# A retention-plus-MLP kernel whose order is laid out by a planner: new rule for fetched TensorE instructions, new table of moves, a bank-marking matmul moved to the head of its group, and another gate for w_out

## The chip, the cores and the metric

The kernel runs on one core of one Trainium2 chip. The metric is the device time of one execution in microseconds (us); the median of three runs before the change is 287.15 us (286.87 to 288.31). Engines are called PE (TensorE, the matrix engine), PEld (its weight loads, which overlap its matmuls), DVE (VectorE), ACT (ScalarE), POOL (GpSimd) and SP (SyncE, which here issues transfers only). Lines are named as in the kernel before: L983 is line 983.

## The reference

Inputs are float32: q, k and v of shape 8 x 8 x 576 x 64 (batch, heads, positions, width), w_in 512 x 2048 and w_out 2048 x 512. The output is 4608 x 512 in float32.

```python
scores = (1/sqrt(64)) * q @ k.transpose            # per batch and head
gamma  = 1 - 2 ** (-5 - head)
ret    = scores * where(row >= col, gamma ** (row - col), 0)
x      = (ret @ v) laid out as 4608 tokens x 512   # heads side by side
h      = x @ w_in                                  # 4608 x 2048
out    = (h * cos(h)) @ w_out                      # 4608 x 512
```

## The kernel before

**Units of attention.** The 576 positions of a batch are cut into units of 256 positions (four chunks of 64) and a remainder of 64. For one unit the kernel loads q, k and v into staging tiles (`stgq`, `stgk`, `stgv`; `load`, L537), scales or casts them to bf16 (`qnat`, `natk`, `natv`; `unit`, L548), turns q and k round (`tpe` on PE for the first four units, a transposing DMA, `txb`, for the others), makes masked scores inside the chunks and a running state across them (`scores`, `states`, `snap`), and from both the unit's rows of x, in bf16, in `xt` (`outputs`, L734). All these are short matmuls of 64 rows, and all of them are recorded at L650.

**Blocks of the MLP.** The 4608 tokens make nine blocks of 512; two units fill one block. For blocks 0 to 3 the first product is plain (`mlp1`, matmuls at L854). For blocks 4 to 8 it is one level of a Strassen-Winograd scheme with seven products in place of eight (`seven1`, matmuls at L983, four groups per block, 20 in all). The second product takes that scheme for all nine blocks (`wino2`, matmuls at L1123). h * cos(h) is made by ACT (cosine) and by DVE or POOL (product), L863 to L866 and L966 to L972.

**A group of `seven1`.** It holds three of the eight PSUM banks: A, Bb and C. Product 1 is accumulated in A. Then ACT copies A to Bb (`seed`, L912, recorded at L914), and product 2 adds onto that copy in Bb. For the adding to work, a matmul must have written the whole of Bb as its last use; the list `whole` keeps for each bank whether that is so. Where it isn't, `mark` (L471, recorded at L472) puts one matmul of ones of 512 columns on that bank, ahead of ACT's copy. The copy waits for it.

**What sets the order.** `graph` (L1180) lists some 1,400 tasks, each with an engine, a duration by estimate, and a due time. `shift` (L217) adds to the due times a table of corrections, `SHIFT` (L370): each three characters of it are a step to the next task that is moved, and a move of up to 40 us either way. `run` (L235) then plays the tasks on five engines in estimated time, and takes at each step a task that can start soonest and has the smallest due time; this gives the order in every queue, and the banks and buffers. So each engine's queue on the chip is a fixed list, and waits are by semaphores. A slot of a pool of buffers (`bk` is the PSUM banks) is picked at L333: the one that came free first.

**The fetch of PE's instructions in the planner.** `pick` has a rule (L270 to L273): PE's instructions come in blocks of 256; a block is asked for when PE has come to a certain instruction (128 + 256k, L326), and PE can't pass instruction 443 + 256k before `FETCH` = 6500 ns have gone by since then. `count` is a task's number of PE instructions, `seen` their running sum. L324 adds what `warm` (L475) will issue: matmuls of ones that fill PE's gaps early in the kernel.

**Loads of weights.** `load_w` (L832) issues from POOL's queue, four loads for each of w_in and w_out. Those of w_out wait for a load of the unit (1, 1) (L1229): its q. In the task list a unit loads k, q, v in this order, save the first two units (q, k, v).

```python
gate = [(st["q", (1, 1)], 0)]                        # L1229
for x in range(4):
    self.load_w("wout", x, gate, 200 + x)            # L1231
self.unit((2, 0), gate=[("wout", 2, 0)])             # L1232
```

Of the kernel before, what the change touches and what calls it, by code (L numbers as in the profile page):

```python
# [11 lines left out]
B, H, S, D = 8, 8, 576, 64  # L12
# [3 lines left out]
NR = S // CH  # L16
# [94 lines left out]
class Task:  # L111
    @property
    def allocs(self):
        return [b for b in self.bufs if b.slot is None]

    __slots__ = ("eng", "dur", "parts", "deps", "succ", "wait", "bufs", "start", "prio", "fix", "dma",
                 "port", "name", "order", "late", "ops", "tail", "count", "then")


LAT = {"pe": 215, "act": 220, "dve": 180, "pool": 110, "sp": 60}  # L120
# [10 lines left out]
class Graph:  # L131
# [13 lines left out]
    def add(self, eng, dur, parts, prio=None, alloc=(), dma=None, port=False, name="", late=0.0, tail=1700, count=0):  # L145
        t = Task()
        t.eng, t.dur, t.parts, t.dma, t.port, t.name = eng, dur, parts, dma, port, name
        t.fix, t.prio, t.succ, t.start, t.late, t.tail, t.count, t.then = prio, None, [], None, late, tail, count, None
        deps = {}

        def dep(other, end):
            if other is not t:
                deps[other] = max(deps.get(other, 0), end)

        bufs = dict.fromkeys(alloc)
        for end, fn, r, w, kw in parts:
            for k in r:
                for o, x in self.wr.get(k, []):
                    dep(o, x)
            for k in w:  # L160
                for o, x in self.rd.get(k, []) + self.wr.get(k, []):
                    dep(o, x)
            for k in r:
                self.rd.setdefault(k, []).append((t, end))
            for k in w:
                self.wr[k], self.rd[k] = [(t, end)], []
            for k in list(r) + list(w):
                if isinstance(k[0], Buf):
                    bufs[k[0]] = 1
        t.bufs = list(bufs)  # L170
        for b in t.bufs:
            if not b.tasks and b.pool in self.fifo:
                self.fifo[b.pool].append(b)
            b.tasks.append(t)
            b.left += 1
        t.deps = list(deps.items())
        for o, _ in t.deps:
            o.succ.append(t)
        t.wait = len(t.deps)
        self.tasks.append(t)  # L180
        return t

    ENTER, LEAVE, BOND = 95, 105, 2000

# [50 lines left out]
    def run(self):  # L235
        self.reset()
        free = {e: 0.0 for e in ("pe", "act", "dve", "pool", "sp")}
        ready = {e: [] for e in free}
        seen, asked = 0, {}
        dma_free, port_free = 0.0, {"dve": 0.0, "pool": 0.0}  # L240
        est, order, last, mode, held = {}, [], None, "", None
        for t in self.tasks:
# [18 lines left out]
        def pick(e):  # L261
            cand = []
            for t in ready[e]:
                if e == "pe" and held and t is not held and (t.then or t.name[:3] != "ses"):
                    continue
                a = slots(t)
                if a is None:
                    continue
                s = max(free[e], est[t], a)
                if e == "pe" and t.count:  # L270
                    k = (seen + t.count - 443) // 256
                    if k >= 0 and 443 + 256 * k > seen and k in asked:
                        s = max(s, asked[k] + self.FETCH - t.dur * (443 + 256 * k - seen) / t.count)  # L273
                if t.port:
                    s = max(s, port_free["pool" if e == "dve" else "dve"])
                if t.dma is not None and e != "pool":
                    s = max(s, dma_free - self.BACKLOG)
                cand.append((s, t))
            if e == "pe" and not held:
# [3 lines left out]
                if due:  # L283
                    d = min(due, key=lambda t: t.prio)
# [10 lines left out]
        n = 0  # L295
        while n < len(self.tasks):
            best = None
            for e in free:
                c = pick(e)
# [6 lines left out]
            s, t = best  # L306
            e = t.eng
            if e == "pe":
                s = max(s, free[e] + self.switch(mode, t.name))
# [11 lines left out]
            if e == "pe":  # L321
                mode = t.name
                held = t.then or (held if t is not held else None)
                if gap > 400 and s < 45000:  # L324
                    seen += 2 * self.fill(gap, seen)
                k = (seen + t.count - 128) // 256  # L326
                if k >= 0 and k not in asked:
                    asked[k] = s + t.dur * max(0, 128 + 256 * k - seen) / max(1, t.count)
                seen += t.count
            for b in t.allocs:  # L330
                pool = self.pools[b.pool]
                ok = [i for i, f in enumerate(pool) if f is not None and f <= s + 1e-6]
                i = min(ok, key=lambda i: pool[i])  # L333
                b.slot, pool[i] = i, None
                if b.pool in self.fifo:
                    self.fifo[b.pool].remove(b)
                self.holder[b.pool][i] = b
            done = s + t.dur
            if t.dma is not None:
                dma_free = max(dma_free, s + (2400 if e == "pool" and s > dma_free - 700 else 1700 if e == "pool" else 1150)) + t.dma  # L340
# [19 lines left out]
class Kernel:  # L360
# [6 lines left out]
    FORDER = [0, 1, 2, 3, 8, 9, 10, 11, 4, 5, 6, 7, 12, 13, 14, 15]  # L367
    SPLIT = 1
    SEVEN = (4, 5, 6, 7, 8)
    SHIFT = (  # L370
        "#)wC+`CYP1b1*[N,o\\$Aw$;o(jh$=J$NX&1G%lH%Ki*n<*nr+yi;kv&Db&rV)n;&]),8$&j.%<B$C|.?c0`-)[%$U%'<@&&h(:a"
        ")p5'?1&Uo&,t)/.&4y&T3&6`&Q,&,#(mp$;8&E8&]F%g1*3U&$u&eZ/'e&8l,Z6$\\'$T6$YK$X|(Y,(Ow'h0$/b(xT&nP$*o&<<"
        "(AI=Y`$',.MgE|K)|GDYyGMV$?:&)i$@6&KL(4P'#U$4(&5D$K3D0{&$f)Ds/GW&lX*q(((r2H?%1K$v5'rq&<I(Wx*PB+7<,$Z"
        "%yE%>v&i`=qx%in'c*$q.*o1(\\|%r=*W\\;OX*eL&2mQf#(Wx&ci*uH.{R&v_*{W%X\\)vv'ie'V],{Y+lH+:1&9#%?c2'k;y$07Y"
        "*j[&wv'$6(Mn$>$)&^$(91_I$=X(yg'9g)lB$jm*bo+M7*{V/q36E[&W;$[N11n),1.1d&<-)BH,.F&{L$k7.|K't-&@A+{G5Vj"
        "@;T$+H&=5&,M,\\=(%J%(T$uTJ)s'c^+Bt$fV&qR$c'%mT&u($c[%`o'#f)dK5as&lJ$c{$,7$4v)$j$)w5df2;S(835)7%K*'.B"
        '*-X?9=&VG&`T&_]&^O+f?2*3'
    )
    TXENG = ("pool", "dve", "pool", "dve")
    COARSE = ((2, 0), (3, 0))  # L380
    HALVES = (0, 2)
# [155 lines left out]
    def load(self, which, u, rows, gate, fast):  # L537

        stg = self.staged[which, u] = Buf("stg" + which)
        src = self.src["qkv".index(which)]  # L540
        for i, (p0, n, o, ny, b, r0) in enumerate(rows):
            at, w = (b * H * S + r0) * D, ny * D
            self.one("sp", 500, lambda e, p0=p0, n=n, o=o, w=w, at=at: e.dma_start(  # L543
                ap(self.at(stg), 1024, p0, n, o, [w, H], [1, w]), bass.AP(src, at, [[w, n], [S * D, H], [1, w]])),
                r=gate, w=[(stg, i)], sem=lambda i=i: f"{which}{stg.slot}_{i}", dma=1840 if ny == 2 else 600 * n // 64, tail=720 if fast else 1800)
        return stg

    def unit(self, u, fast=False, gate=()):  # L548
# [4 lines left out]
        for which, nat, dst in [todo[i] for i in ((1, 0, 2) if fast else (0, 1, 2))]:  # L553
# [6 lines left out]
            stg = self.load(which, u, rows, gate, fast)  # L560
            nb = t[nat] = Buf(nat)
            for y in range(2):
                rs = [(stg, i) for i in ((y,) if fine else range(len(rows)))]

                def out(y=y, nb=nb):
                    return ap(self.at(nb), 1024, 0, 128, 512 * y, [256, 2], [64, 4], [1, D])
# [4 lines left out]
                def inp(stg=stg, o=o, hs=[[n * w, c] for n, c in hs]):  # L571
                    return ap(self.at(stg), 1024, 0, 128, o, *hs, [1, D])
                if which == "k":
                    eng = ("act", "pool")[y] if fast else "pool"
                    self.copy(eng, {"act": 520, "dve": 610, "pool": 580}[eng], out, inp, rs, [(nb, y)])
                else:
                    tab, key = (self.WV, "wv") if which == "v" else (self.WQ, "wq")
                    col = 32 if rem else 40 * fine + 16 * u[1] + 8 * y
                    eng = "dve" if fast and which == "q" else "pool"
                    self.one(eng, 610 if eng == "dve" else 1030, lambda e, out=out, inp=inp, tab=tab, col=col, hs=hs: e.tensor_tensor(  # L580
                        out(), inp(), ap(tab, NT, 0, 128, col, *hs, [0, D]), ALU.mult),
                        r=rs + [(key,)], w=[(nb, y)], port=eng == "pool")
# [329 lines left out]
    def seed(self, src, dst):  # L912

        self.one("act", 490, lambda e: e.activation(self.at(dst).ap(), self.at(src).ap(), AF.Copy),  # L914
                 r=[(src,)], w=[(dst,)], seed=dst)

    def seven1(self, j, g, prio, span):

# [58 lines left out]
        for n, p in enumerate((1, 5, 2, 6, 7, 3, 4)):  # L977
            l, rr, keys, bank, first = spec[p]

            def mm(e, l=l, rr=rr, bank=bank, first=first):  # L980
                for f in range(2):
                    for c in range(2):
# [2 lines left out]
                return inst  # L985

            self.one("pe", 4 * 109, mm, r=keys + [("g1", j, g) if p != 1 else ("g3",)], w=[(bank,)] + [("g1", j, g)] * (p == 1) + [("g3",)] * (p == 3),
                     alloc=[gt] + [A, Bb] * (p == 1), whole=(bank,), prio=prio + span * n / 7, name=f"M{p}_{j}", count=8.4)
            if p == 1:
                self.seed(A, Bb)  # L990
            elif p == 2:
# [188 lines left out]
    def graph(self):  # L1180
# [37 lines left out]
        self.unit((1, 0), True)  # L1218
        attend((1, 0), 2000, 10)
        st, base = self.staged, T1  # L1220
        for x, which, pr in ((0, "q", 100), (2, "q", 101), (1, "k", 102), (3, "k", 103)):
            self.load_w("win", x, [(st[which, (min(x, 1), 0)], 0)], pr)
        self.unit((0, 1), gate=[("win", 2)])
        attend((0, 1), base - 8000, 2000)
        self.unit((1, 1))
        for i, f in enumerate(self.FORDER):
            for ses in ((0,), (1,)) if f // 4 in self.HALVES else ((0, 1),):
                self.mlp1(0, f, ses, T0 + 435 * (2 * i + ses[0]))
        gate = [(st["q", (1, 1)], 0)]  # L1229
        for x in range(4):  # L1230
            self.load_w("wout", x, gate, 200 + x)  # L1231
        self.unit((2, 0), gate=[("wout", 2, 0)])  # L1232
# [62 lines left out]
```

## Time and profile before

| what | value |
|---|---|
| median of three runs | 287.15 us |
| the profiled execution's own time | 287.54 us |
| its span, first to last instruction | 285.8 us |
| PE busy | 273.3 us (96%), 4094 matmuls |
| DVE, ACT, POOL busy | 225.3, 174.8, 152.7 us |
| granted TensorE clock | 1.000 |
| DMA queue of PE's instructions (q8) | 32 packets, 0.52 MB |
| first matmul, end of the last one | 1.12 us, 282.66 us |

The profile is of one execution, whose own time lies 0.39 us over the median of the runs; 1.7 us of it lie outside the span. Busy time of PE holds matmuls that overlap: the profile models their ends, so a matmul of 256 columns has 273 ns as its own duration, and yet eight of them in a row take 0.87 us from start to start. The text therefore takes the time from one start to the next.

### The profile page before, as it was taken

What the parts mean: (1) busy time and instruction counts of PE and PEld (TensorE: products, weight loads), DVE (VectorE), ACT (ScalarE), POOL (GpSimd) and SP (SyncE); (2) the same over time, 40 slices, a digit from 0 to 9 for tenths busy, and PEclk for the clock granted to TensorE, in tenths of its full rate; (3) what the DMA queues carried; (4) which work ended last, traced back from release to release, by engine and by line L of the source; (5) the groups of instructions that cost most, each with busy time, mean ns of one, the idle gap of its engine ahead of it and who ended that gap; (6) DMA issues with size and microseconds to landing.
All of it is one profiled execution on the core that took longest, in us unless ns stands there. A gap on an engine that the chain in (4) does not pass through costs nothing.

```text
span 285.8 us, 9725 instructions
## 1 busy us (share of the span) xinstructions
PE 273.3 (96%) x4094; PEld 215.7 (75%) x4094; DVE 225.3 (79%) x387; ACT 174.8 (61%) x357; POOL 152.7 (53%) x170
## 2 busy tenths in 40 slices
PE   6789999899999899999999999999999999999995
PEld 2467577788874575677888887888888978888884
DVE  3677779899958769968868988889897987867752
ACT  5347776442456556544568777695779667488520
POOL 5452970449464526086599577883785333136400
PEclk9999999999999999999999999999999999999999
DMA  7999999999999999999999999898494000120115
GB/s 198 268 218 280 240 190 262 278 207 173 201 160 267 182 205 265 217 202 178 282 188 204 164 242 257 202 207 192 102 168 128 3 5 0 68 81 2 75 39 184
DMA packets 133131, 49.91 MB, mean 175 GB/s; under 512 B 105440, under 2 KB 128992, under 8 KB 133088
## 3 DMA queue, kind: packets, MB, share of 16 engines
q1 hardware_dynamic: 128576, 44.84, 73.4%
q0 software_dynamic: 4224, 4.19, 9.2%
q8 instruction: 32, 0.52, 0.8%
q10 hardware_dynamic: 288, 0.26, 0.3%
q14 instruction: 11, 0.09, 0.1%
HBM read 36.70 MB, written 9.44 MB: 161 GB/s over the span
## 4 chain that ended last, share of the span: by engine, by line
PE 80%; DMA 12%; POOL 4%; issue 1%; SPq 1%; ACT 0%; DVE 0%; POOLq 0%
PE bk L1123 39%; PE bk L983 22%; PE bk L854 12%; PE bk L650 7%; DMA stgv<-in_v_dram 6%; DMA wout<-in_moe_w_out_dram 4%; DMA win<-in_moe_w_in_dram 3%; POOL natv L580 2%; POOL wout L838 1%; SPq L543 1%; POOL qnat L580 1%; POOL natk L534 0%; PE bk L472 0%; ACT sn L533 0%; ACT bk L914 0%
## 5 line engine op out<-in xcount | busy, mean ns | idle before, releaser
L972 POOL TENSOR_TENSOR gt<-sq,cb 128x512 bf16<-128x512 f32 x40 | 46.1, 1157 | 42.7 <-ACT cb L968 22.2
L854 PE MATMUL bk<-xt,win 128*128 128x256 bf16 (+1 forms) x352 | 61.3, 321 | 0.9 <-ACT xt L533 0.7
L863 ACT ACTIVATE cb<-bk 128x256 bf16<-128x256 f32 (+1 forms) x88 | 41.7, 482 | 29.4 <-PE bk L854 26.1
L866 DVE TENSOR_TENSOR gt<-bk,cb 128x256 bf16<-128x256 f32 (+1 forms) x88 | 45.4, 540 | 16.7 <-ACT cb L863 16.5
L580 POOL TENSOR_TENSOR natv<-stgv,wv 128x512 bf16<-128x512 f32 x36 | 37.5, 1049 | 25.7 <-DVE s L1054 9.2
L854 PEld LDWEIGHTS bk<-xt,win 128*128 128x128 bf16 x352 | 33.2, 98 | 19.8 <-ACT xt L533 1.5
L580 POOL TENSOR_TENSOR qnat<-stgq,wq 128x512 bf16<-128x512 f32 x32 | 33.8, 1064 | 26.6 <-DVE s L1060 9.8
L1123 PE MATMUL bk<-wout,gt 128*128 128x256 bf16 x288 | 36.6, 273 | 1.3 <-issue 1.0
L972 DVE TENSOR_TENSOR gt<-bk,cb 128x512 bf16<-128x512 f32 x40 | 27.1, 687 | 12.2 <-ACT cb L968 12.2
L1123 PE MATMUL bk<-tw,s 128*128 128x256 bf16 x288 | 36.0, 273 | 0.0
L1123 PE MATMUL bk<-wout,s 128*128 128x256 bf16 x288 | 35.8, 273 | 0.0
L983 PE MATMUL bk<-xt,win 128*128 128x256 bf16 x240 | 34.6, 273 | 0.7 <-ACT bk L914 0.7
L966 DVE TENSOR_TENSOR sq<-bk,sq 128x512 f32<-128x512 f32 x40 | 27.0, 686 | 6.3 <-PE bk L983 3.2
L689 DVE TENSOR_TENSOR pt<-bk,tr 128x512 bf16<-128x512 f32 x48 | 30.8, 683 | 1.5 <-PE bk L650 1.1
L1123 PEld LDWEIGHTS bk<-wout,gt 128*128 128x128 bf16 x288 | 27.6, 98 | 5.1 <-issue 1.2
L1123 PEld LDWEIGHTS bk<-tw,s 128*128 128x128 bf16 x288 | 27.9, 98 | 4.0
L1123 PEld LDWEIGHTS bk<-wout,s 128*128 128x128 bf16 x288 | 27.5, 98 | 4.6 <-DVE s L1060 0.5
L968 ACT ACTIVATE cb<-sq 128x512 bf16<-128x512 f32 x40 | 25.1, 631 | 9.3 <-DVE sq L966 8.9
L534 POOL CAST natk<-stgk 128x512 bf16<-128x512 f32 x34 | 20.8, 629 | 16.8 <-DVE s L1054 12.0
L968 ACT ACTIVATE cb<-bk 128x512 bf16<-128x512 f32 x40 | 23.6, 600 | 6.5 <-PE bk L983 5.5
L983 PEld LDWEIGHTS bk<-xt,win 128*128 128x128 bf16 x240 | 22.9, 98 | 4.1 <-ACT bk L914 1.1
L533 ACT ACTIVATE sn<-bk 128x512 f32<-128x512 f32 (+1 forms) x29 | 16.2, 567 | 15.7 <-PE bk L1123 15.7
(82 smaller groups left out, 424.9 us busy)
## 6 DMA issues: line engine op xcount, KB each, us to landing
out_dram<-os SPq DMA_DIRECT2D x16, 512.0 KB, 4.6
stgk<-in_k_dram SPq DMA_DIRECT2D x20, 256.0 KB, 5.2
stgq<-in_q_dram SPq DMA_DIRECT2D x20, 256.0 KB, 4.9
stgv<-in_v_dram SPq DMA_DIRECT2D x20, 256.0 KB, 4.9
stgq<-in_q_dram SPq DMA_DIRECT2D x6, 512.0 KB, 7.1
stgk<-in_k_dram SPq DMA_DIRECT2D x6, 512.0 KB, 9.0
stgv<-in_v_dram SPq DMA_DIRECT2D x6, 512.0 KB, 7.4
win<-in_moe_w_in_dram POOLq DMA_DIRECT2D x4, 512.0 KB, 8.6
```

Source lines behind the costliest of these rows:

```text
L534: return self.one(eng, dur, lambda e: e.tensor_copy(dst(), src()), r=r, w=w, port=eng == "pool", **kw)
L580: self.one(eng, 610 if eng == "dve" else 1030, lambda e, out=out, inp=inp, tab=tab, col=col, hs=hs: e.tensor_tensor(out(), inp(), ap(tab, ...
L650: return lambda e: e.matmul(out(), lhs(), rhs(), start=start, stop=True, skip_group_check=True)
L689: self.one("dve", 610, lambda e, r=r, b=b, pt=pt: e.tensor_tensor(ap(self.at(pt), 1024, 0, 128, 512 * r, [64 * ny * ny, 8 // ny // ny], [1 ...
L854: inst = e.matmul(ap(self.at(bk), 512, 0, 128, 0, [1, n]), ap(self.WIN, 4 * DFF, 0, 128, c * DFF + 128 * f, [1, 128]), ap(self.at(xt), 204 ...
L863: self.one("act", n - 15, lambda e: e.activation(ap(self.at(cb), TB, 0, 128, 0, [1, n]), ap(self.at(bk), 512, 0, 128, 0, [1, n]), AF.Sin, ...
L866: self.one("dve", 75 + n / 0.96, lambda e: e.tensor_tensor(ap(self.at(gt), NF * TB, 0, 128, f * TB + 256 * h0, [1, n]), ap(self.at(bk), 51 ...
L966: self.one("dve", 610, lambda e: e.tensor_tensor(half(src), self.at(bank).ap(), half(src), ALU.add), r=[(bank,)], w=four(src))
L968: self.one("act", 530 if name else 490, lambda e: e.activation(self.at(cb).ap(), ap(self.at(src), size, 0, 128, 0, [1, 512]), AF.Sin, bias ...
L972: self.one(eng, 1120 if name else 610, lambda e: e.tensor_tensor(ap(self.at(gt), NF * TB, 0, 128, (8 * n + 2 * g) * TB + 256 * h, [TB, 2], ...
L983: inst = e.matmul(ap(self.at(bank), 512, 0, 128, 256 * f, [1, 256]), l(c, f), rr(c), stop=True, skip_group_check=True, start=(first and f ...
L1123: inst = e.matmul(place(bank, tt), l(f, tt), rr(f), stop=True, skip_group_check=True, start=(first and f == 0 and tt < len(bank)))
```

## The change

1. The planner's fetch rule: in place of the 6500 ns, a time that depends on when the block was asked for (`fetch`). The running count starts at 20 and not at 0, counts a seven1 product as 8.0 instructions and not 8.4, and takes the number of gap-filling matmuls as the emission itself does.
2. The bank mark: `mark` is now issued ahead of product 1 of the group and no longer ahead of ACT's copy, and Bb gets its bank first (`[Bb, A]` for `[A, Bb]`), a bank that is already `whole` if one is free.
3. w_out's loads wait for the k load of unit (1, 1), not for its q load (`GATE`).
4. `SHIFT` is replaced. The old table moves 206 tasks, the new one 232; 82 tasks stand in both, none with the same move. The size of the middle move is 21.8 us in the old table and 26.0 us in the new one; the largest is 40 us in both.
5. Staging tiles have four keys whatever the number of loads, so that a later load into a slot waits for all readers of the earlier one. `CASTS` (empty), `SLABS` and `NEXT` are names for what was written out before; of the four loads of w_in, the last comes behind the loads of unit (0, 1) in the list of tasks.

```diff
+        t.seed = next((p[4]["seed"] for p in parts if "seed" in p[4]), None)
+        t.marks = [(k[0], 1 if k[0] in kw.get("whole", ()) else 2 if k[0] in kw.get("more", ()) else 0)
+                   for end, fn, r, w, kw in parts if eng == "pe" for k in w if isinstance(k[0], Buf) and k[0].pool == "bk"]
...
+    @staticmethod
+    def fetch(at):
+        return 11500 if at < 30000 else 10000 if at < 55000 else 8500 if at < 100000 else 7200 if at < 205000 else 6200
...
-        seen, asked = 0, {}
+        seen, asked, whole = 20, {}, [False] * 8
...
-                        s = max(s, asked[k] + self.FETCH - t.dur * (443 + 256 * k - seen) / t.count)
+                        s = max(s, asked[k] + self.fetch(asked[k]) - t.dur * (443 + 256 * k - seen) / t.count)
...
-                if gap > 400 and s < 45000:
-                    seen += 2 * self.fill(gap, seen)
+                if gap > 400 and s < 40000:
+                    seen += 2 * max(1, self.fill(gap, s - gap))
...
-                i = min(ok, key=lambda i: pool[i])
+                i = min(ok, key=lambda i: (b is t.seed and not whole[i], pool[i]))
...
+            for b, kind in t.marks:
+                whole[b.slot] = kind == 1 or (kind == 2 and whole[b.slot])
...
+    CASTS = {}
+    SLABS = ((0, 'q', 0, 100), (2, 'q', 1, 101), (1, 'k', 1, 102), (3, 'k', 1, 103))
+    NEXT = 2
     SHIFT = (
...
+    GATE = 'k'
...
+            keys = range(4) if ny == 2 else (2 * i, 2 * i + 1) if n == 128 else (i,)
...
-                r=gate, w=[(stg, i)], sem=lambda i=i: f"{which}{stg.slot}_{i}", dma=1840 if ny == 2 else 600 * n // 64, tail=720 if fast else 1800)
+                r=gate, w=[(stg, j) for j in keys], sem=lambda i=keys[0]: f"{which}{stg.slot}_{i}", dma=1840 if ny == 2 else 600 * n // 64, tail=720 if fast else 1800)
...
-                rs = [(stg, i) for i in ((y,) if fine else range(len(rows)))]
+                rs = [(stg, i) for i in ((2 * y, 2 * y + 1) if fine else range(4))]
...
-                 r=[(src,)], w=[(dst,)], seed=dst)
+                 r=[(src,)], w=[(dst,)])
...
-                     alloc=[gt] + [A, Bb] * (p == 1), whole=(bank,), prio=prio + span * n / 7, name=f"M{p}_{j}", count=8.4)
+                     alloc=[gt] + [Bb, A] * (p == 1), whole=(bank,), seed=Bb if p == 1 else None, prio=prio + span * n / 7, name=f"M{p}_{j}", count=8.0)
...
-        for x, which, pr in ((0, "q", 100), (2, "q", 101), (1, "k", 102), (3, "k", 103)):
-            self.load_w("win", x, [(st[which, (min(x, 1), 0)], 0)], pr)
-        self.unit((0, 1), gate=[("win", 2)])
+        for x, which, u, pr in self.SLABS[:3]:
+            self.load_w("win", x, [(st[which, (u, 0)], 0)], pr)
+        self.unit((0, 1), gate=[("win", self.NEXT)])
+        for x, which, u, pr in self.SLABS[3:]:
+            self.load_w("win", x, [(st[which, (u % 2, u // 2)], 0)], pr)
...
-        gate = [(st["q", (1, 1)], 0)]
+        gate = [(st[self.GATE, (1, 1)], 0)]
```

## The prediction

> **What bounds the kernel now.** I read the page first: engines, then the slices.
>
> ```profile
> span 285.8 us, 9725 instructions
> PE 273.3 (96%) x4094; PEld 215.7 (75%) x4094; DVE 225.3 (79%) x387; ACT 174.8 (61%) x357; POOL 152.7 (53%) x170
> ...
> PE   6789999899999899999999999999999999999995
> ...
> DMA  7999999999999999999999999898494000120115
> ...
> q8 instruction: 32, 0.52, 0.8%
> ```
>
> PE is the bound from slice 4 on; its clock is granted in full, so no clock enters. The DMA engines are full for the first 200 us, and PE's own instructions come through them: 32 packets of 16 KB, one per 256 instructions.
>
> Then the chain that ended last, asked around the places where PE is not on it:
>
> ```profile
> 52.24 0.55 PE bk L1123 x5
> 52.79 1.01 issue
> 53.81 0.49 PE bk L1123 x3
> ...
> 95.65 0.68 PE bk L650 x60
> 96.33 1.12 issue
> 97.46 0.35 PE bk L650 x20
> ...
> 229.72 1.30 PE bk L650 x121
> ...
> 234.44 0.23 PE bk L472
> 234.67 0.02 issue
> 234.69 0.59 ACT bk L914
> 235.28 0.05 issue
> 235.33 1.48 PE bk L983 x12
> ```
>
> "issue" is a stop that no semaphore explains. I set it beside the packets of the instruction queue: the packets for these two places landed at 52.49 and 95.95, and PE went on 1.3 and 1.5 us later (53.81, 97.46). A third stop hides in the L650 run at 229.72: landing 229.66, PE again at 231.02. Counting every row of PE's queue (weight load, matmul, wait), all three stops stand behind rows 1472, 2752 and 7360, which leave the same remainder, 192, on division by 256. They are late fetches. The last lines are another stop: the mark at 234.28 came late, ACT's copy waited for it, PE for the copy.
>
> To see what holes there are in all, I took the timeline of PE from start to start and subtracted the steady step (0.109 us for 256 columns: eight L1123 in 0.87). From 21.2 us on, what is over 0.15 us:
> - fetch: 1.18 (52.5), 1.31 (96.1), 0.19 (230.8): 2.68 us;
> - mark: 0.84 at 234.3, besides three marks of 0.22 each: 1.50 us;
> - work not yet there, 33 to 49 us: 0.39, 0.43, 0.39, 0.18, 0.40 and a 0.21 inside L650, and three gap fillers of 0.21 (35.6 to 38.5): 2.6 us;
> - scattered: 0.18, 0.47, 0.32: 1.0 us;
> - 33 visits to the short matmuls (L650), whose entries and exits cost 8.0 us, 0.24 each.
>
> Everything else is matmuls at their steady pace. Before 21.2 us PE waits for the first loads, and after 282.7 the last rows are copied and stored (3.1 us); no part of the change is aimed at either.
>
> **The change, part by part.** *Fetch rule.* It adds no instruction; it moves tasks on PE's queue so that clusters of short matmuls don't outrun a fetch. From the ask (instruction 128 + 256k) to the resumption the three stops took 11.0 us (asked at 42.8), 9.3 (88.2) and 5.8 (225.2). The old rule charged 6.5 throughout, so the planner couldn't see the first two. The new one charges 10.0, 8.5 and 6.2 there: 1.0 and 0.8 short, 0.4 long. So back come 2.7 us at best, and 0.9 (2.7 less 1.0 and 0.8) if both blocks again run at the rule's edge; I take 2.0. The work that follows the stops is PE's own and ready, so the gain goes through to the end.
>
> The Trainium skill has a rule against this term: Runtime: NRT & Kernel Launch, section Instruction fetch mechanics, says that fetch is mostly hidden, a crossing costing one DMA tail-bump. The trace disagrees with it at three of 32 blocks (2.68 us) and agrees at the other 29; by the page this term would be nothing and the sum 2.0 us higher.
>
> *Mark.* At the head of product 1 the mark is done before ACT's copy can start (product 1 itself must end first), so its wait goes:
>
> ```profile
> engine op xcount: duration ns min/median/max, first and last start us, forms
> L472 PEld LDWEIGHTS bk<-one x3: 97/97/98, 172.6 to 234.2; 128*128 128x128 bf16 x3
> L472 PE MATMUL bk<-one x3: 379/379/379, 172.7 to 234.3; 128*128 128x512 bf16 x3
> ...
>   ACT bk L914: 2.9, 3
> ```
>
> ACT waited 2.9 us for three marks, yet PE stopped for one copy alone. PE gains that 0.84, and 0.22 for each mark which the choice of a whole bank saves: 0 to 1.5 us, I take 0.9 (the stop, and no mark counted on). What could eat it: a mark at the head waits there for Bb's last reader, and product 1 is queued behind it; the planner already books Bb from product 1 on in both kernels, so I cost that at nothing, and at 0.84 for each place where the estimate is off.
>
> *w_out's gate.* Three loads of w_out were issued at 32.48, just behind the natv products (30.49 to 32.53); q of (1, 1), issued at 23.95, had landed by 31.95 (8.0 us). So the gate was open 0.5 us before POOL came to it: in the present order it binds nothing. SP issued k of (1, 1) behind it, at 26.97, and POOL cast it from 34.75: were SP's order kept, the k gate would open up to 2.8 us later than the q gate. In the task list k stands before q, and the new table decides. Behind the waiting load on POOL are the casts of (1, 1), from 34.75, and behind them PE's scores and SP's next loads, which wait for free staging tiles. w_out is 4.2 MB at some 245 GB/s, 17 us of full DMA (239 and 251 GB/s in 20 to 40 and 40 to 60 us); moved ahead it delays q, k and v by as much. PE's cover is block 0's second product, which needs of the loads w_out alone (14 half-products of 0.87, 12 us). Ends: a gain of 2.6 (all holes of 33 to 49 filled), a loss of 2.8. Near the middle, by the row that says the gate was open: a gain of 0.3.
>
> *New table.* No entry survives, so every place is laid anew. The known ends: two visits fewer to the short matmuls, a gain of 0.5; against it, holes at the 20 hand-offs of seven1 (L914), each worth the 0.84 seen once. With a quarter of them, 4.2. I take a loss of 1.0, the scattered holes once more.
>
> *Keys, SLABS, counts.* Loads of one unit go down SP's queue in order, and the first already waits for the readers of the slot's old content; the further keys add waits that are over by then: nothing, and with that order gone at most the 0.6 of one cast (L534). The fourth w_in load (issued with the third at 15.33) moves in the list only; its cost lies inside the w_out bounds. The counts steer the fetch rule.
>
> Sum: 2.0 + 0.9 + 0.3 - 1.0 = 2.2 us gained. From the profiled execution's 287.54 that is 285.34; that execution is 0.39 over the median, so against the median: 287.15 - 2.2 = 284.95, say **285.0 us**. With every end at its best the gain is 2.7 + 1.5 + 2.6 + 0.5 = 7.3; at its worst the loss is 4.2 + 2.8 - 0.9 = 6.1.
>
> **The rivals.**
> 1. *Holes traded.* The fetch stops go (2.0) and the mark's (0.9), but the new layout has its own. For it: four further blocks landed only 2.0 to 3.0 us before their need (need at 19.2, 37.2, 109.3, 187.5), so with 1.4 us from landing to use 0.6 to 1.6 us is to spare; an order laid anew can pull other clusters forward. Against it: the rule now sees them. New holes of 2.5 in place of 1.0: 286.5 us.
> 2. *Hand-offs of seven1 bind: slower.* Where seven1 runs beside wino2, DVE is busy in 85 to 90% of these two stretches and ACT in 73 to 75% (columns after the stretch: its length, then busy us of PE, PEld, DVE, ACT, POOL):
>
> ```profile
> 157.00:177.00 20.00, 19.70 (x348) 16.74 (x345) 18.08 (x30) 14.53 (x30) 13.23 (x14) 1.00 1.18 223
> 177.00:197.00 20.00, 20.00 (x360) 17.23 (x350) 16.95 (x26) 15.04 (x32) 15.79 (x17) 1.00 0.94 202
> ```
>
> PE is hardly short there now (19.70 and 20.00 of 20), since each copy (0.58 us) has other work before its product 2. A table that puts two groups closer, or takes banks at the wrong moment, lays 0.84 open per hand-off. The gains without the new holes are 3.2 us, so it decides from four of 20 on; with seven, 287.15 - 3.2 + 7 x 0.84 = 289.8 us. For it: nothing of the old layout is kept, and ACT waits for L983 at ten of 20 copies (5.9 us). Against it: the planner prices this wait already, and the present order shows one such stop.
> 3. *Fetch is not cured*: the stops recur elsewhere (the new figures are below two of the three waits measured). Only 0.9 + 0.3 - 1.0 is gained: 286.95 us. The page's rule would lead here as well.
> 4. *All goes well*, w_out included: 2.7 + 0.9 + 1.5 (over half of the holes of 33 to 49) - 0.5 = 4.6 gained, 282.5 us.
>
> **How the numbers follow.** Forecast 0.46 (its own range 283.3 to 285.7), rival 1 0.21, rival 2 0.22, rival 3 0.05, rival 4 0.06. Half a per cent, 1.4 us, is about what measurement tells from no change: 285.7 to 288.6. Faster: forecast and rival 4, 0.52. Same: rivals 1 and 3, 0.26. Slower: rival 2, 0.22. The range goes from 282.6, leaving out half of rival 4, to 289.8, leaving out the upper half of rival 2: about 0.14 outside.
>
> **What would show it.** Fetch right: no "issue" pieces near 1 us in the chain, and every packet of the instruction queue landing over 1.4 us ahead of its block. Mark right: no wait of L914 on L472. Gate: the first load of w_out issued before 32.5 us, and smaller PE holes from 33 to 49. Table: PE idle before L983 and L1123 after 137 us no more than now (1.0 us by the groups' rows, 0.7 of it behind L914). I am wrong if holes at L914, L968 or at wout sum to over 3.2 us, or if the number of visits to L650 grows by more than a few.

## The result

The changed kernel takes 284.47 us (median of four runs, 283.85 to 284.95) where the kernel before takes 287.73 beside it: a ratio of 0.9886, 95% interval 0.9847 to 0.9926. A second comparison of the same two kernels gave 0.9879 (0.9859 to 0.9898). The forecast was 285.0 us, 0.9925 of 287.15; the direction was right and the gain about a half larger than forecast.

The profiled execution fell from 287.54 to 284.38 us, its span from 285.8 to 282.6. The page of the changed kernel, engines, slices of PE, instruction queue and chain:

```profile
span 282.6 us, 9717 instructions
PE 274.2 (97%) x4093; PEld 216.6 (77%) x4093; DVE 224.0 (79%) x387; ACT 175.5 (62%) x357; POOL 151.8 (54%) x170
...
PE   7889989999999999999999999999999999999995
...
q8 instruction: 32, 0.52, 0.8%
...
PE 93%; DVE 3%; DMA 1%; ACT 1%; issue 0%; DVEq 0%
```

Busy time of each engine is within 1.3 us of what it was; the work is the same. The slices of PE are full from slice 7 on. PE holds 93% of the chain that ended last; in the kernel before it was:

```profile
PE 80%; DMA 12%; POOL 4%; issue 1%; SPq 1%; ACT 0%; DVE 0%; POOLq 0%
```

Most of that rise is no gain in itself. Before, the chain reached 49.0 us through loads (DMA and POOL), and now it reaches that time through PE; of the gain only "issue", 1% to 0%, is seen here.

The chain of the changed kernel at the three places where the chain of before had its stops, around 53, 96 and 230 us:

```profile
52.68 0.44 PE bk L871 x4
53.12 0.87 PE bk L1140 x8
53.99 1.06 PE bk L667 x64
...
93.94 0.91 PE bk L667 x80
94.85 1.83 PE bk L871 x8
...
228.71 1.34 PE bk L667 x128
230.05 2.73 PE bk L1140 x24
```

No "issue" piece is left, though the same clusters of short matmuls (L667, which was L650) are there, 80 and 128 in a row. In the packets of the instruction queue, every block landed at least 1.9 us before row 443 + 256k of PE's queue was reached. PE's queue has 8302 rows in both kernels and so reaches 31 such borders (k from 0 to 30); the last of the 32 packets isn't needed by a row that the profile shows.

ACT's copy in the groups of seven1 (L914 before, L931 now), who made it wait:

```profile
L931 ACT ACTIVATE bk<-bk x20: 580/582/619, 133.1 to 257.5; 128x512 f32<-128x512 f32 x20
...
  PE bk L1000: 6.9, 11
  DVE s L1071: 1.9, 1
```

One mark is left of three (142.8 us), and no copy waits for it. PE waits for no copy either.

Where the time went, from one matmul's start to the next, as in the prediction; the first 21.2 us apart:

| us | before | after |
|---|---|---|
| stops for a fetch | 2.68 | 0 |
| marks, and the stop behind one | 0.65 + 0.84 | 0.21 |
| early holes and gap fillers (to 49 us) | 1.99 + 0.65 | 1.58 + 0.86 |
| scattered holes over 0.15 | 0.97 | 0.54 |
| entries and exits of L650 / L667, up to 0.15 each | 6.82 (33 visits) | 7.47 (35 visits) |
| inside the visits | 4.99 | 5.33 |
| matmuls at their steady pace, rest | 241.51 | 241.99 |
| up to 21.2 us | 20.18 | 20.12 |
| sum, first to last matmul's start | 281.27 | 278.10 |

The first two rows give 3.96 us of gain; the others take 0.8 back. The prediction's 8.0 us for the 33 visits are not the 6.82 of this table, in part because they hold two of the early holes too (0.40 and 0.43, which lie at the edge of a visit).

### The profile page after: what moved, and what is told of

Read it like the earlier page. It is cut to its first block, busy times and chain, and to the rows that moved or that the text cites. A ratio compares the mean times of both kernels' runs of the same rounds, so it can differ in the third digit from the quotient of the medians.

```text
span 282.6 us, 9717 instructions
## 1 busy us (share of the span) xinstructions
PE 274.2 (97%) x4093; PEld 216.6 (77%) x4093; DVE 224.0 (79%) x387; ACT 175.5 (62%) x357; POOL 151.8 (54%) x170
## 4 chain that ended last, share of the span: by engine, by line
PE 93%; DVE 3%; DMA 1%; ACT 1%; issue 0%; DVEq 0%
PE bk L1140 40%; PE bk L1000 22%; PE bk L871 19%; PE bk L667 10%; DVE pt L706 2%; DMA stgq<-in_q_dram 1%; PE bk L621 1%; PE bk L492 1%; ACT cb L880 1%; DVE gt L883 0%; DVE kt L548 0%; DVE qnat L597 0%; ACT xt L547 0%; ACT natk L547 0%; ACT qt L547 0%
## 5 line engine op out<-in xcount | busy, mean ns | idle before, releaser
L883 DVE TENSOR_TENSOR gt<-bk,cb 128x256 bf16<-128x256 f32 (+1 forms) x88 | 46.3, 542 | 10.9 <-ACT cb L880 7.9
L597 POOL TENSOR_TENSOR natv<-stgv,wv 128x512 bf16<-128x512 f32 x36 | 37.2, 1042 | 31.6 <-DVE s L1077 8.2
L871 PEld LDWEIGHTS bk<-xt,win 128*128 128x128 bf16 x352 | 33.1, 98 | 20.2 <-ACT xt L547 1.3
L1140 PE MATMUL bk<-wout,gt 128*128 128x256 bf16 x288 | 35.7, 273 | 0.0
L1129 DVE TENSOR_TENSOR os<-bk,sn 128x512 f32<-128x512 f32 (+1 forms) x28 | 18.6, 668 | 10.8 <-PE bk L1140 10.7
```

Of the source, the lines that this page charges most:

```text
L871: inst = e.matmul(ap(self.at(bk), 512, 0, 128, 0, [1, n]), ap(self.WIN, 4 * DFF, 0, 128, c * DFF + 128 * f, [1, 128]), ap(self.at(xt), 204 ...
L883: self.one("dve", 75 + n / 0.96, lambda e: e.tensor_tensor(ap(self.at(gt), NF * TB, 0, 128, f * TB + 256 * h0, [1, n]), ap(self.at(bk), 51 ...
L1140: inst = e.matmul(place(bank, tt), l(f, tt), rr(f), stop=True, skip_group_check=True, start=(first and f == 0 and tt < len(bank)))
```

## The experiments

Theory: the gain is made of the fetch stops and the marks, and the new table by itself gives nothing. Rivals: the stops belong to the work at those places and not to the fetch; the marks lie beside other work; the earlier gate of w_out is what gained. Rule and table can't simply be exchanged: with the new table and the old rule the planner comes to a point where each free task needs a buffer that another one holds, and gives no order at all, and neither does the changed kernel with the old table. The kernel before with the new rule and the old table does get an order, 9 us longer by the planner's own estimate; no run of it was made. So the runs don't tell apart what the rule and what the table did. I moved the fetch borders instead, which shows what the stops are.

### Moving the borders: the kernel before with 24 and 54 more rows

The first filling of a gap is nine matmuls of 512 columns on ones. Cut into narrower ones, it puts more rows in PE's queue and leaves the columns; every later border of a block then falls on other work.

```diff
-            for _ in range(n):
+            first, self.begun = not getattr(self, "begun", False), True
+            for i in range(n):
+                if first and i < 4:                 # 9 for 54 more rows
+                    for x in range(0, 512, 128):
+                        m = min(128, 512 - x)
+                        inst = e.matmul(ap(self.at(self.wb), 512, 0, 128, x, [1, m]), self.ONE.ap(), ap(self.ONE, 128, 0, 128, 0, [1, m]),
+                                        start=True, stop=True, skip_group_check=True)
+                    continue
```

> Kernel before; four of the nine first gap-filling matmuls of 512 columns are each split into four of 128, so that 24 more rows stand at the head of PE's queue for the same columns; nothing else changes. Fetch theory (a stop comes where row 448 + 256k of the queue is reached before its block has landed for 1.4 us): the block borders fall on other work. Slid along the trace of before, the stop at 52.5 us stays, about 1.4 us, at about 51 us, and those at 96.1 and 230.8 vanish: 2.7 us of stops become 1.4, span 284.5. Rival (the stops belong to the work at these places, by a wait that the profile doesn't show): all three stay at the same instructions, span 285.8.

Measured: ratio 0.9984 (0.9958 to 1.0009), span 286.9 in the profile, which is of the longest of ten executions. The chain at its three stops:

```profile
51.73 0.55 PE bk L861 x5
52.27 1.07 issue
53.34 0.92 PE bk L861 x7
...
95.94 1.18 POOL natk L541 x2
97.12 0.73 issue
97.85 0.44 PE bk L657 x32
...
187.47 0.60 PE bk L657 x57
188.07 0.73 issue
188.80 0.32 PE bk L657 x14
```

All three stand behind rows 448 + 256k (k = 4, 9, 21; in the kernel before k = 4, 9, 27), and so the first two behind work 24 rows earlier: the first no longer inside L1123 but inside L854 (here L861). The stop at 230.8 is gone, and a new one of 0.92 us came at 187.9. That is the fetch theory; the rival is out. The working beforehand had two of the places right, the stop at 52 us and the one at 230.8 that goes; the stop at 96 us was to vanish and didn't, and the new one wasn't foreseen. So the sizes were missed: 1.23 + 1.07 + 0.92 = 3.2 us, not 1.4. The block for 96 us took 9.9 us from its ask to landing where it took 7.8 before, and the one for 188 us took 6.6 in place of 3.9: I had slid the borders along and kept the times of the fetches.

> Kernel before; all nine first gap-filling matmuls are split into four of 128 columns: 54 more rows at the head of PE's queue, same columns. Fetch theory: stops of about 2.4 us near 49.7 and 1.5 us near 100, both behind rows with the remainder 192 on division by 256, none at 96 or 231; 2.7 us become about 4, span 286.8 to 287.3. Rival (the work at these places): unchanged, span 285.8.

Measured: ratio 1.016 (1.0114 to 1.0207), span 290.8. Three stops of 1.0 us, at 48.0, 55.2 and 101.3 us, all behind rows 448 + 256k, none at 96 or 231. The rule for the places held; of the two stops expected (2.4 us near 49.7, 1.5 near 100), the first came as two, 3.0 us in all where 4 were expected. The loss comes from the start: PE is 5.0 us behind the kernel before at 27.7 us, ahead of all three stops, and 4.9 at the end. The timeline of POOL and PE there, and the granted clock in the slices of the page:

```profile
20.51 2.04 POOL L587 TENSOR_TENSOR natv<-stgv,wv 128x512 bf16<-128x512 f32 x2 [2.42 <-DMA stgv<-in_v_dram]
...
22.70 0.44 PE L657 MATMUL bk<-natv,natk 64*64 64x64 bf16 x16 [2.81 <-POOL natv L587]
...
PEclk9997999999999999999999999999999999999999
```

The load of v came 3.7 us later than in the kernel before (its use began at 16.82 there), PE stood idle for 2.81 us, and the clock fell for a while (0.7 in the fourth slice). Why the load was late isn't settled, so this kernel says something of the stops' places alone.

### Moving the borders in the changed kernel

The same edit there, with ten matmuls of 47 columns and one of 42 in place of each of the nine (180 rows), and with four cut into four (24 rows).

> Changed kernel; the nine first gap-filling matmuls of 512 columns are each split into eleven (ten of 47, one of 42): 180 more rows at the head of PE's queue, same columns. Fetch theory: the new order is free of stops only by where its borders lie; one comes back, about 0.9 us, near 111 us, and perhaps 0.15 near 157: span 283.4 to 283.7. Rival (the new order has no cluster that can outrun a fetch, wherever the borders lie): no stop, 282.6.

Measured: ratio 1.0128 (1.0086 to 1.0169), span 288.5. The chain:

```profile
112.22 0.50 PE bk L674 x47
112.72 1.52 issue
114.24 0.19 PE bk L674
...
125.02 0.15 PE bk L674 x4
125.18 0.63 issue
125.81 0.54 PE bk L674 x44
...
161.02 1.09 PE bk L1007 x9
162.11 1.10 issue
163.21 0.50 PE bk L1007 x3
```

The stops are back in the new order, 1.71, 0.84 and 1.26 us, all behind rows 448 + 256k; a further 1.2 us at 40.4 has its block's landing (40.20) 1.46 us before PE went on, but the trace puts w_out's landing at 41.15 as well. Set against the changed kernel instruction by instruction, the delay is 1.73 us at 43 us, 4.25 at 138, 5.66 at 168 and 5.87 at the end, so with them the gain is lost. The new order owes its freedom from stops to where the borders fall on it: the planner's row count and the table belong together. The size was missed again (0.9 expected). The block behind the stop at 125 us took 12.2 us from ask to landing, where the rule charges 7.2; the one behind the largest stop took only 5.2, but PE came from its row 128 to its row 448 in 5.1.

> Changed kernel; four of the nine first gap-filling matmuls are each split into four of 128 columns: 24 more rows at the head of PE's queue, same columns. Fetch theory, with the margins that the blocks of the changed kernel have (each landed 1.9 us or more ahead of row 443 + 256k, 1.4 from landing to use): the borders move by 24 rows, which is at most 1.3 us of work, so no stop over 0.2 us comes back, span 282.3 to 283.2. Rival (the order is free of stops only at exactly its own border, any shift brings them back): stops of 0.5 us and more, span over 283.5.

Measured: ratio 0.9885 (0.9860 to 0.9909), as the changed kernel itself. One small stop stands behind a row 448 + 256k (k = 23), 0.22 us, where none over 0.2 was expected; its block landed at 197.26, 1.53 us before PE went on. The chain there:

```profile
198.47 0.28 PE bk L674 x20
198.75 0.04 issue
198.79 0.41 PE bk L674 x20
```

So the order has some room, as the fetch theory says; in this execution it was used up at one place, by a block that took 7.1 us from ask to landing (4.8 in the changed kernel). The execution that was profiled was the longest of its six, 285.5 us of span, by holes of another kind. The timeline of POOL and PE:

```profile
201.20 1.36 POOL L555 CAST natk<-stgk 128x512 bf16<-128x512 f32 x2 [3.42 <-DMA stgk<-in_k_dram]
...
207.97 3.38 POOL L996 TENSOR_TENSOR gt<-sq,cb 128x512 bf16<-128x512 f32 x3
...
209.81 0.61 PE L1007 MATMUL bk<-xt,win 128*128 128x256 bf16 x4 [1.50 <-ACT sq L554]
```

A late load holds up POOL's queue, the products behind it hold their `sq` tiles, ACT waits for one, and PE for ACT. That is how this order lost time in this one execution; that the other long ones are of this kind isn't shown.

### The mark alone

> Kernel before, same order in every queue; only the three marking matmuls are issued ahead of product 1 of their group and not ahead of ACT's copy. Mark theory: ACT's 2.9 us of waits for the mark go below 0.5, the stop of 0.84 at 234.3 goes, span 285.0. Rival (the copy then waits for product 1 or for ACT itself as long): PE still stops 0.5 or more before L983 near 235, span 285.6 to 285.8.

```diff
+                head = kw.pop("head", None)
+                if head is not None and not whole[head.slot]:
+                    self.mark(head)
+                    whole[head.slot] = True
...
-                     alloc=[gt] + [A, Bb] * (p == 1), whole=(bank,), prio=prio + span * n / 7, name=f"M{p}_{j}", count=8.4)
+                     alloc=[gt] + [A, Bb] * (p == 1), whole=(bank,), head=Bb if p == 1 else None, prio=prio + span * n / 7, name=f"M{p}_{j}", count=8.4)
```

Measured: span 285.0. The waits of ACT's copy and the chain around the place:

```profile
  PE bk L987: 6.1, 11
```

```profile
232.27 0.44 PE bk L987 x4
232.71 0.21 PE bk L476
232.92 0.87 PE bk L987 x8
233.80 0.87 PE bk L1127 x8
234.67 1.31 PE bk L987 x12
```

The mark stands before the group, and the stop behind it is gone. Instruction by instruction, this kernel runs within 0.25 us of the kernel before from 55 to 230 us, save at a moved mark (0.4 at 171), and ends 0.83 ahead. The times alone (0.9981, 0.9956 to 1.0006) wouldn't show it.

> Changed kernel with part 2 undone: the mark again ahead of ACT's copy, A first and any bank; the order of the queues is otherwise the same, with five marks in place of one. Mark theory: four more marks of 0.22, 0.9 us, and a copy or two that comes late for product 2, 0.8 each: span 283.5 to 285.1. Rival (marks and their waits lie beside other work): at most 0.3, span up to 282.9.

```diff
-                     alloc=[gt] + [Bb, A] * (p == 1), whole=(bank,), seed=Bb if p == 1 else None, prio=prio + span * n / 7, name=f"M{p}_{j}", count=8.0)
+                     alloc=[gt] + [A, Bb] * (p == 1), whole=(bank,), prio=prio + span * n / 7, name=f"M{p}_{j}", count=8.0)
...
-                 r=[(src,)], w=[(dst,)])
+                 r=[(src,)], w=[(dst,)], seed=dst)
```

Measured: ratio 0.9942 (0.9924 to 0.9961), span 284.3. The mark, and who waited for it:

```profile
L486 PE MATMUL bk<-one x5: 379/379/379, 144.4 to 235.4; 128*128 128x512 bf16 x5
...
  ACT bk L931: 8.3, 5
```

Five marks, 8.3 us of waiting by ACT, and one new hole of 0.32 (148.4). Against the changed kernel it is 0.5 us behind at 43 us (in that execution w_out landed later) and 1.7 at the end: 1.2 us for part 2 as a whole, 0.87 of it the four marks. No copy came late for product 2, which the mark theory had expected once or twice (0.8 each): in this order ACT's waits for the marks lie beside other work of PE.

### The gate alone

Only the wait is exchanged; the queues keep their order.

```diff
             for end, fn, r, w, kw in t.parts:
+                if w and w[0][0] == "wout" and t.dma is not None:
+                    r = [(self.staged["q", (1, 1)], 0)]      # "k" in the kernel before
```

> Changed kernel, the same order in every queue; only the wait of w_out's loads is for the q load of unit (1, 1) and not for its k load. SP now issues that k at 25.4 and that q at 26.8. Gate theory: the first load of w_out moves from 32.4 to about 34.6 us, the first product of L1140 (39.9) waits for it about 1.5 us, part of which the hole at 42.4 gives back: span 283.6 to 284.1. Rival (POOL's order decides, the gate is open anyway): 282.6.

Measured: span 282.8, ratio 0.9916 (0.9891 to 0.9941). The timeline of POOL, first in the changed kernel, then with the q gate:

```profile
32.37 2.29 POOL L855 DMA_DIRECT2D wout<-in_moe_w_out_dram  x3
...
35.65 0.81 POOL L855 DMA_DIRECT2D wout<-in_moe_w_out_dram  x1
```

```profile
33.85 2.29 POOL L857 DMA_DIRECT2D wout<-in_moe_w_out_dram  x3 [1.36 <-DMA stgq<-in_q_dram]
...
37.14 0.81 POOL L857 DMA_DIRECT2D wout<-in_moe_w_out_dram  x1
```

The q gate holds POOL for 1.36 us, and PE still ends only 0.13 us behind. The rival's time was right, though not its reason: the gate does hold POOL, but the first load of w_out, issued 1.48 us later, lands only 0.55 us later (39.74 for 39.19), still 0.33 us ahead of its first product at 40.07. Here the gate is worth next to nothing. The profiled execution is the fastest of its six; by the medians beside the kernel before (0.9916 for the changed kernel's 0.9886 and 0.9879, with intervals that overlap) up to 1 us isn't excluded.

> Kernel before, the same order in every queue; only the wait of w_out's loads is for the k load of unit (1, 1), which SP here issues behind the q load. Gate theory: the first load of w_out moves from 32.5 to between 33.5 and 34.7, and the hole before L1123 at 49.0 grows by 1 to 2 us: span 286.8 to 287.8. Rival (w_out is early enough): 285.8.

Measured: ratio 1.0071 (1.0046 to 1.0096), span 288.0. In the old order SP issues q first, so the k gate opens late:

```profile
33.81 2.29 POOL L840 DMA_DIRECT2D wout<-in_moe_w_out_dram  x3 [1.66 <-DMA stgk<-in_k_dram]
```

The hole at 49.0 grew by 0.9, as the gate theory says, but the fetch stop at 52.5 took this back whole: PE came to that border later, and the block was there. The lasting 2.2 us come later, at 63, 67, 77 and 97 us (0.3, 0.6, 0.8, 0.3). POOL's casts run 1.3 us later in this kernel, and at 77 us PE waits for a product of DVE's (`s`), at 97 for a fetch; that the late casts are behind these holes fits, but isn't shown step by step. So the later of the two gates costs 2.2 us in the old order and 0.13 in the new one.

> Changed kernel with part 3 undone in the planner too: the gate is the q load, and the order is laid out anew with the same table. The gate alone would cost the planner a start of w_out later by 2.2 us: span 283.5 to 285. If the table's moves fit only the order they were found with, new holes come all over the kernel and the span is over 285.

```diff
-    GATE = 'k'
+    GATE = 'q'
```

Measured: ratio 1.0268 (1.0244 to 1.0293), span 293.4. From 21.2 us on there are 33 holes over 0.15 us, 14.0 us together, in place of 5 with 2.1; they lie all over the kernel, up to 1.8 each, and two of them (0.45 at 95.8, 0.81 at 156.9) stand behind rows 448 + 256k; at the second the profile names a copy of ACT's as well. The gate's own cost is 0.13, so nearly all of it is the table meeting an order that it was not found with. The planner's own estimate of this order is 13 us longer, too.

### The changed kernel again

> The changed kernel once more, unedited, beside the kernel before on the same chip, for a narrower interval: between 0.985 and 0.992 of the time before, and no stop of the fetch kind; if the stops had only been spared by luck in the first profile, some profile shows one of 0.3 us or more behind a row with the remainder 192.

Measured: 0.9879 (0.9859 to 0.9898), span 281.7, no fetch stop, the same holes at the same instructions as in the first profile (1.00, 0.38, 0.25, 0.27), and 1.0 us less at the start (by 16 us). So the start alone can differ by 1.0 us between two executions of this kernel.

## Why the prediction was right

*Fetch rule*: 2.0 us taken, 2.68 measured in the trace. The stops were late fetches, as forecast, and the border experiments show it: stops go with the row number, not with the work. The term was undersized because I left 0.7 for blocks at the rule's edge; in the changed kernel no block is there, the closest having landed 1.9 us before its row 443. That it was the rule, and not the table that came with it, which took the stops away is argued and not shown. The rule doesn't ensure it either: with 180 more rows at its head the same order has three stops again, with 24 one of 0.22. So the whole 2.68 came back partly by where the borders happen to fall. The rule of the page Runtime: NRT & Kernel Launch (section Instruction fetch mechanics) in the Trainium skill, that a crossing is mostly hidden, holds at all 31 borders that the changed kernel's queue reaches and at 28 of the 31 of the kernel before (the prediction has 29 of 32). Rival 3, which took that rule up, is out.

*Mark*: 0.9 taken, 1.28 measured. The stop of 0.84 went, as the kernel before with the mark moved alone shows; undersized is the choice of a whole bank, on which I didn't count: it saved two marks (0.44).

*Gate*: 0.3 taken; the early holes and fillers fell by 0.2 (2.64 to 2.44), and the gate exchanged alone is worth 0.13. That the two numbers are close is luck, for the holes are others: a new one of 1.00 us at 37.2 takes the place of most of the old ones. The first load of w_out moved by 0.1 us only, from 32.48 to 32.37, since POOL's queue ahead of it decides: this "binds nothing" was right. What moved is the fourth load, and the order on POOL moved it, not the gate. Before, it stood behind five casts and products:

```profile
38.88 0.81 POOL L838 DMA_DIRECT2D wout<-in_moe_w_out_dram  x1
```

It landed at 48.89, and PE stood for it in the hole at 49.0 (0.40); issued at 35.65 in the changed kernel, it landed at 47.70, 1.3 us ahead of its use, and that hole is gone. In return the first product with w_out now comes at 39.93 us where it came at 45.27, and the first load is hardly ahead of it: by 0.7 us in this profile, 0.05 in the second one, and in the kernel with part 2 undone PE stood 1.5 us for it. The fear that k would be behind q came out otherwise, for the new table makes SP issue k first (25.44, q at 26.80). The bound that I had given for that case, a loss of up to 2.8, was well founded in size: in the old order it costs 2.2, though none of that is left of the wait for w_out itself.

*New table*: a loss of 1.0 taken. Measured is 1.0, which is luck, for it is made of other things than I had named: not more scattered holes (0.97 to 0.54), but two more visits to the short matmuls (0.65 + 0.34) and 0.4 more steady work left after 21.2 us, which probably belongs to the start of that one execution.

The sum was -2.2 and came out -3.2; the bounds for each term held. Rival 1 (new holes for old) and rival 2 (hand-offs of seven1 bind) are out for this order: scattered holes fell, and PE waits for no copy at L931. Rival 4 (all goes well, w_out included) had the fetch right, but the early holes gave 0.2 and not 1.5. In the kernel laid out anew with the q gate, copies at L931 do hold PE up; the rows of who waited for them:

```profile
  PEld bk L1000: 2.2, 4
  PE bk L1000: 1.1, 4
```

From start to start, as the 0.84 was taken, these four stops are 0.40, 0.40, 0.54 and 0.40 us: rival 2's kind of loss is real where the table doesn't fit, at half the price that I gave it.

## What to carry to other kernels

In a kernel whose bound engine runs a fixed list, a stop that no semaphore explains should be set against the row number in that engine's queue: three stops with the same remainder on division by 256 point to a late fetch, and cutting an early, idle filler into more rows moves the borders and tests it. An order laid out by a planner, its rule and its table of corrections are one piece: undoing a part that by itself is worth next to nothing cost 11 us when the order was laid out anew. Judge small edits instruction by instruction in the trace; 0.84 us of 286 were plain there and not in the times.

## What the runs showed of the hardware

- From landing of a block of PE's instructions to PE going on, 1.3 to 1.6 us passed at each of thirteen stops in five kernels.
- How long a block takes from its ask to landing varies widely. The ask is taken at row 128 + 256k, as the planner has it; no run shows where it really stands. In the kernel before it took 9.7 us (block 4) and 3.0 (block 7) with the DMA engines full, and 2.3 (block 24) and 4.5 (block 27) with their busy share at 0.03 or less. So the stop at 230.8 (block 27) fell while the DMA engines were nearly idle: PE ran from its row 128 to its row 448 in 5.6 us there. The longest time is 12.2 us, with the engines full.
- It changes from one kernel to the next at the same time (block 9, asked at 86 to 88.5 us: 7.8 in the kernel before, 9.9 and 12.2 with 24 and 54 more rows, 4.0 in the changed kernel), so a rule by time alone, like `fetch`, is a guess that fits one order.
- In the kernel with 54 more rows PE was idle for 2.81 us up to 22.7 us. The granted clock stayed at 1.00 until 24.4, was 0.50 from there to 27.8, with matmuls of 256 columns 0.21 us apart and not 0.109, and then 1.00 again. A wait of 1.5 us, in the changed kernel with 24 more rows, had no such effect. The Trainium skill, TensorE: Matmul & The Clock Gate, Part 1, tells of half the clock after an idle window of some 3.4 us; the halving agrees, but the idle time ahead of it here was shorter, 2.81 us.
